# An attention and two expert layers in one kernel: a longer hand-set order, queries turned in other banks, and routings spread over their periods

## The chip, the core and the metric

The kernel runs on one core of a Trainium2 chip. The metric is the device time of one execution in microseconds (us), and less is better. The core has four engines that compute: TensorE (PE in the profile, with its weight loads listed apart as PEld), VectorE (DVE), ScalarE (ACT) and GpSimd (POOL). SyncE (SP) mostly issues transfers. Each engine runs its own instructions strictly in the order of its queue and waits at semaphores for the others.

## The reference, cut to what matters

A recurrent attention over 4 batches, 8 heads, 768 steps and 48 values to a head is followed by two layers of experts over the 3072 tokens that come out of it. Each token goes to one of eight experts; nothing is dropped.

```python
for t in range(768):                       # for every batch and head
    y[:, :, t] = r[t] @ (state + outer(u * k[t], v[t]))
    state = w[t][:, None] * state + outer(k[t], v[t])

x = y, heads side by side: 3072 tokens x 384
# layer 1: the router is a cosine
logits = normed(x) @ normed(expert_emb).T / tau
e = argmax(logits); gate = softmax(logits)[e]
x = gate * (relu(x @ w1[e]) @ w2[e])       # 384 -> 1024 -> 384
# layer 2: the router is linear, with a sigmoid gate on top
e = argmax(x @ w_gate); gate = softmax(x @ w_gate)[e]
out = gate * sigmoid(x @ w_output_gate)[e] * (relu(x @ m2w1[e]) @ m2w2[e])
```

## The kernel before, in words

**Attention.** Two heads of one batch make a pair, so there are 16 pairs, g = 0 to 15. Steps lie 6 to a partition. The decays of a pair are turned by six TensorE transposes (`turned`, L590, tile ptw), copied by ScalarE into a padded tile ws (L598), and VectorE runs two product scans over ws, Q (L604) and P (L606): running products of the decays inside chunks of 128 steps. Keys are turned (ptk) and divided by Q into K, queries are turned (ptr) and multiplied by P into R (`scaled`, L616). K scaled by the product of a chunk is Kh (L624). Scores pa = R'Kh (L635) are masked into A (L641), chunk states ps (L658) are chained into sa (L661), the outputs py (L673 with A, L677 with the states) and the bonus term cv give the token rows x (L682). The bonus is cb (L558, a sum of the products rk), which goes to HBM and comes back turned as ct (L559 to L561, cd is its place in HBM), and cv is v times ct on GpSimd (L574).

**Periods.** The pairs are worked on in periods that overlap three pairs. `period(i)` (L759) turns and scans the decays of pair i+1, makes the scores and states of pair i, and finishes the outputs of pair i-1. `period(-1)` is the start, periods 0 to 15 are full ones, and period 16 finishes the last pair. In this text Q(n) is the scan Q of pair n, so that period i runs from the start of Q(i+1) to the start of Q(i+2). The PSUM banks have tags: px (2 banks: everything turned), pa00, pa01, pa40, pa41 (scores, also used for the cosine's turn), py (outputs).

**Router of layer 1.** Whenever 96 columns of x are ready for a batch, the squares of x are summed by ScalarE (`squares`, L691, tile jk), x is turned (L705) and multiplied with the experts' directions (pl, L712), and VectorE adds that into the logits L (L718, L720). After the fourth pair of a batch `route1` (L722) makes the inverse norms on GpSimd (a pow), scales the logits, picks the expert, counts places with a scan and two matmuls (`route`, L311, tile pp), and writes an entry for each token into HBM by six indirect transfers of GpSimd (`scatter`, L367, from the tile ent). For the batches 0 to 2 this lies in periods 5 and 6, 9 and 10, 13 and 14.

**Handover.** `largest` (L406) ranks the experts of the first three batches, the entries of the two first windows are fetched (`entries`, L390, tile first), the raw first weights of the first expert follow (`raw_u`, L397, tile ur_first, four quarters, two buffers), token rows are gathered by indirect transfers (xr, L983), and each weight is split into two parts: a rounded one by ScalarE (uh, vh, L382) and the rest by GpSimd or VectorE (ul, vl, L384).

**Experts.** A unit is a window of up to 512 tokens of one expert. Its matrix products take three passes over the rounded and remaining parts: ph (L1015) in the first product, pz (L1037 and L1048) in the second. Units follow from the handover to the end of the kernel.

**What sets the order.** From the start to the end of period 16 the order of every engine's instructions is that of the code (`tc.manual_schedule`, closed by `order.close()`); from the last batch's routing and the first unit on a scheduler orders, with `queue_behind(x, y)` keeping x behind y.

## Time and profile before

| what | value |
|---|---|
| time, median of 3 runs | 812.99 us (811.99 to 816.59) |
| the profiled execution: own time, span | 808.58 us, 806.9 us |
| TensorE busy | 729.5 us, 90% of the span |
| VectorE busy | 452.9 us, 56% |
| ScalarE busy | 340.6 us, 42% |
| GpSimd busy | 361.5 us, 45% |
| mean granted TensorE clock | 0.941 of full speed |

The span is what the profiler saw between the first and the last instruction; the execution's own time is longer by what lies around it, 1.7 us. An engine's share of busy time is a mean over stages that differ: the attention, the handover and the experts each have their own, and the experts' stage is the longest.

Three views are shown below. A row of a timeline has the start in us, the length in us, the engine and line, the instruction as output <- inputs with sizes, how many follow one another as one row, and in brackets the idle time of the engine ahead of it and what ended that. A row of busy time by stretch has from:to, the length of the stretch, then the busy us (and instructions) of PE, PEld, DVE, ACT and POOL, and last the granted TensorE clock, the share of transfer engines that were busy, and GB/s. The tile view has the instructions that touch one tile, shortest/middle/longest in ns, first and last start.

### The profile page before, as it was taken

To read this page: it belongs to the slowest core of one execution; us is meant where nothing else is said; L and a number is where in the kernel's file an instruction comes from. 1 tells how busy PE (TensorE), PEld (TensorE's weight loads), DVE (VectorE), ACT (ScalarE), POOL (GpSimd) and SP (SyncE) were. 2 spreads that over 40 slices of the span, in tenths; PEclk is the share of its full clock that TensorE was granted. 3 is DMA by queue.
4 is the path that set the end of the run, shared out by engine and by line. 5 is a ranking of instruction groups with operands and counts; after the bars stand their busy time and mean duration, and the time that the engine had idled before them with its cause. 6 is when DMAs were issued, how large, how long until landed. Compare 5 with 4: busy or idle time off the path is not lost.

```text
span 806.9 us, 14112 instructions
## 1 busy us (share of the span) xinstructions
PE 729.5 (90%) x4964; PEld 693.5 (86%) x4964; DVE 452.9 (56%) x1251; ACT 340.6 (42%) x789; POOL 361.5 (45%) x340
## 2 busy tenths in 40 slices
PE   7589969968967888999999999999899999999995
PEld 6578758867856888999999999998898999999995
DVE  6478757767864367688655755754534242342440
ACT  2244634534532363355534434425255353453541
POOL 3342425426333465366525535415365544445530
PEclk9799968979986599999999999999999999999998
DMA  8855634833200645276543553306266342644430
GB/s 175 154 104 87 151 60 61 174 64 47 75 2 3 191 124 151 86 217 207 177 155 98 181 162 113 129 30 192 73 217 198 112 147 93 195 138 149 151 123 19
DMA packets 184052, 100.52 MB, mean 125 GB/s; under 512 B 129373, under 2 KB 180094, under 8 KB 183972
## 3 DMA queue, kind: packets, MB, share of 16 engines
q1 hardware_dynamic: 175504, 83.11, 38.7%
q0 software_dynamic: 7072, 16.04, 6.9%
q8 instruction: 41, 0.67, 0.4%
q10 hardware_dynamic: 1396, 0.38, 0.2%
q14 instruction: 39, 0.32, 0.1%
HBM read 84.01 MB, written 15.95 MB: 124 GB/s over the span
## 4 chain that ended last, share of the span: by engine, by line
PE 56%; issue 12%; DVE 11%; ACT 9%; POOL 5%; DMA 5%; SPq 1%; POOLq 0%; ACTq 0%; DVEq 0%
PE ph L1015 24%; PE pz L1048 12%; PE pz L1037 10%; DVE Q L604 3%; DMA vr<-in_moe_w_dram 3%; ACT Kh L624 2%; PE pq L1001 2%; PE pt L1068 2%; DVE sa L661 2%; DVE K L616 1%; ACT ws L598 1%; POOL reg L367 1%; PE py L673 1%; PE warm L756 1%; ACT jk L691 1%
## 5 line engine op out<-in xcount | busy, mean ns | idle before, releaser
L384 POOL TENSOR_TENSOR ul<-ur,uh 128x768 fp32r<-128x768 f32 x64 | 118.9, 1859 | 139.1 <-ACT uh L382 136.3
L1022 DVE SCALAR_TENSOR_TENSOR hl<-ph,hh 128x256 fp32r<-128x256 f32 (+11 forms) x152 | 79.4, 523 | 128.2 <-ACT hh L1020 127.1
L1015 PE MATMUL ph<-xl,uh 128*128 128x256 f32 (+11 forms) x432 | 143.1, 331 | 0.2 <-DVE xl L1004 0.2
L1015 PE MATMUL ph<-xh,uh 128*128 128x256 f32 (+11 forms) x432 | 142.1, 335 | 0.7 <-ACT xh L1003 0.6
L1015 PE MATMUL ph<-xh,ul 128*128 128x256 f32 (+11 forms) x432 | 142.1, 329 | 0.0
L1020 ACT ACTIVATE hh<-ph 128x256 fp32r<-128x256 f32 (+11 forms) x152 | 70.1, 462 | 91.6 <-PE ph L1015 91.3
L384 DVE TENSOR_TENSOR vl<-vr,vh 128x768 fp32r<-128x768 f32 x66 | 69.6, 1065 | 37.9 <-ACT vh L382 37.5
L1015 PEld LDWEIGHTS ph<-xh,uh 128*128 128x128 f32 x432 | 82.0, 191 | 2.9 <-ACT xh L1003 0.8
L1015 PEld LDWEIGHTS ph<-xl,uh 128*128 128x128 f32 x432 | 82.6, 191 | 2.0 <-DVE xl L1004 0.5
L1015 PEld LDWEIGHTS ph<-xh,ul 128*128 128x128 f32 x432 | 82.7, 191 | 1.7
L673 PE MATMUL py<-v,A 128*128 128x96 f32 x384 | 65.0, 305 | 15.7 <-DVE x L682 10.2
L382 ACT CAST uh<-ur 128x768 fp32r<-128x768 f32 x64 | 53.4, 834 | 55.5 <-PE ph L1015 33.3
L1037 PE MATMUL pz<-hl,vh 128*128 128x256 f32 (+6 forms) x240 | 75.5, 322 | 0.8 <-DVE hl L1022 0.8
L1048 PE MATMUL pz<-vh,hh 128*128 128x384 f32 (+4 forms) x224 | 75.8, 343 | 0.0
L1048 PE MATMUL pz<-vl,hh 128*128 128x384 f32 (+4 forms) x224 | 73.9, 336 | 0.6 <-DVE vl L384 0.6
L1037 PE MATMUL pz<-hh,vl 128*128 128x256 f32 (+6 forms) x240 | 74.2, 317 | 0.0
L673 PEld LDWEIGHTS py<-v,A 128*128 128x128 f32 x384 | 57.5, 220 | 17.0 <-DVE x L682 10.8
L1037 PE MATMUL pz<-hh,vh 128*128 128x256 f32 (+6 forms) x240 | 71.9, 321 | 0.0
L1048 PE MATMUL pz<-vh,hl 128*128 128x384 f32 (+4 forms) x224 | 71.3, 336 | 0.0
L382 ACT CAST vh<-vr 128x768 fp32r<-128x768 f32 x68 | 56.0, 836 | 31.6 <-DMA vr<-in_moe_w_dram 31.0
L624 ACT ACTIVATE Kh<-K,rta 128x128 f32<-128x128 f32 x96 | 31.6, 399 | 76.2 <-DVE rta L621 76.2
L1004 DVE TENSOR_TENSOR xl<-pq,xh 128x384 fp32r<-128x384 f32 x57 | 30.8, 551 | 36.8 <-ACT xh L1003 32.8
(255 smaller groups left out, 1507.9 us busy)
## 6 DMA issues: line engine op xcount, KB each, us to landing
vr<-in_moe_w_dram SPq DMA_DIRECT2D x68, 384.0 KB, 5.8
ur<-in_moe_w_dram SPq DMA_DIRECT2D x64, 384.0 KB, 3.5
wr<-in_w_dram SPq DMA_DIRECT2D x32, 144.0 KB, 3.4
kr<-in_k_dram SPq DMA_DIRECT2D x32, 144.0 KB, 3.3
rr<-in_r_dram SPq DMA_DIRECT2D x32, 144.0 KB, 3.3
v<-in_v_dram SPq DMA_DIRECT2D x32, 144.0 KB, 3.3
xd<-x SPq DMA_DIRECT2D x4, 1152.0 KB, 5.3
yd<-yr SPq DMA_DIRECT2D x3, 768.0 KB, 5.2
```

The source lines that it names most:

```text
L382: nc.scalar.copy(hi, rw)
L384: eng.tensor_tensor(lo, rw, hi.bitcast(F32), ALU.subtract)
L604: nc.vector.tensor_tensor_scan(Q[:, ::-1], x[:, 2:][:, ::-1], rb[:, ::-1], 0.0, ALU.mult, ALU.max)
L624: nc.scalar.activation(st["Kh", g][:, ck(c)], st["K", g][:, ck(c)], AF.Copy, scale=rt[:, c : c + 1])
L661: nc.vector.scalar_tensor_tensor(sa[:M, z], sa[:M, z - 1], st["pt", g][:M, z : z + 1], ps[:M, z], ALU.mult, ALU.add)
L673: nc.tensor.matmul(p[:, c - c0, h].rearrange("p i d -> p (i d)"), A[:, c, h], V[:, c].rearrange("p h d -> p (h d)"), start=c == c0 and h = ...
L1004: nc.vector.tensor_tensor(xl[:, :, tt], p, xh.bitcast(F32)[:, :, tt], ALU.subtract)
L1015: mm = nc.tensor.matmul(p, self.u[f // 2][x][:, o, 128 * (f % 2) : 128 * (f % 2) + 128], self.xs[y][:, o, :n], start=i == 0, stop=i == 8)
L1020: nc.scalar.activation(hh, p, AF.Relu)
L1022: nc.vector.scalar_tensor_tensor(hl, p, 0.0, hh.bitcast(F32), ALU.max, ALU.subtract)
L1037: nc.tensor.matmul(p, self.v[f // 2][x][:, f % 2, o * 128 : (o + 1) * 128], self.h[f][y], start=i == 0, stop=i == 23)
L1048: nc.tensor.matmul(p[:m], self.h[f][x][:, 128 * t : 128 * t + m], self.v[f // 2][y][:, f % 2], start=i == 0, stop=i == 23)
```

## The change

1. The queries are turned into the score banks pa00 and pa01 where they were turned into px.
2. The check that the decays lie below one (`over_one`, jw, L546) moves on ScalarE from the end of a period to right behind the copies ws.
3. `route1` becomes a generator whose steps `period` calls at five places, with the last of its scatters in the next period (`late`). Division by tau moves into the experts' directions, the small copies of the counts move to ScalarE, and the copies of the choice and the place fall away, since these are written straight into keep and ent.
4. At the start, the transfers of constants leave ScalarE's queue, pair 0's inputs are issued from SP and ScalarE both, constants move behind period -1, the bonus of one pair at a time is worked on, the directions are made in steps over periods 0 to 2, and the transposes without use (`warm`) stand in other places, some now in period 0.
5. At the handover, ranking, entries and raw weights are called inside period 15 (`first_units`, the hook), there are four buffers of raw first weights (two before), and the last batch's turn and routing (`opening`) and the first unit are in the hand-set order too, which closes behind the first unit. Small copies of layer 2's entries wait for the unit's rows; the final check of the decays moves to the end.

```diff
-    def route(which, nm, pool, ppool, ptag, L, T, t0, valid, off, tok):
+    def route(which, nm, pool, ppool, ptag, L, T, t0, valid, off, tok, out=None, pad=None, small=nc.vector.tensor_copy):
...
+        small(carry[which], cu[:, :, T])
...
+        pos = mk[:, :, 1]
...
+    UR = 4
...
-                nc.scalar.dma_start(reg.rearrange("(p t) d -> p t d", p=128), none[:, : RP * E // 128])
...
+                nc.sync.dma_start(reg.rearrange("(p t) d -> p t d", p=128), none[:, : RP * E // 128])
...
-                    nc.sync.dma_start(t[nm][:, :, h, :D], src[b, h0 + h].rearrange("(p j) d -> p j d", j=J))
+                    eng = nc.scalar if g == 0 and h else nc.sync
+                    eng.dma_start(t[nm][:, :, h, :D], src[b, h0 + h].rearrange("(p j) d -> p j d", j=J))
...
-        def turned(g, nm):
+        def turned(g, nm, pool=px_p, tags=("px", "px")):
...
-                p = px_p.tile([128, 3, 128], F32, name=f"pt{nm}{g}_{j0}", tag="px")
+                p = pool.tile([128, 3, 128], F32, name=f"pt{nm}{g}_{j0}", tag=tags[j0 // 3], padded_shape=None if pool is px_p else [128, 4, 128])
...
-        def route1(b, spool, stag):
+        def route1(b, pool, tag, pad=None):
             x, ss, L = st["x", b], st["ss", b], st["L", b]
             s1 = ss[:, 0]
             nc.gpsimd.tensor_tensor(s1, s1, ss[:, 1], ALU.add)
             nc.gpsimd.tensor_tensor(s1, s1, half[:, :NC], ALU.pow)
+            yield
             nc.vector.tensor_scalar(s1, s1, 1e-6, None, ALU.add)
             nc.vector.reciprocal(s1, s1)
-            nc.vector.tensor_scalar(s1, s1, itau, None, ALU.mult)
             nc.vector.tensor_tensor(L, L, b3(s1, E), ALU.mult)
-            gate, oh, ii = yield from route(0, f"a{b}", rt_p, spool, stag, L, NC, b * NC, None, None, None)
             ent = st["ent", b]
-            nc.vector.tensor_copy(ent[:, :, 2], gate)
+            gate, oh, ii = yield from route(0, f"a{b}", rt_p, pool, tag, L, NC, b * NC, None, None, None, ent[:, :, 2], pad, nc.scalar.copy)
             yield
             for c in range(NC):
                 scatter("sc1", reg1, ii[:, c : c + 1], ent[:, c], E * RP1)
...
+        def steps_of(g, n):
+            for i in range(n):
+                next(g, None)
...
-        def period(i, bonus, route=iter(())):
+        def period(i, bonus, route=iter(()), late=iter(()), hook=None):
...
+            steps_of(route, 1)
             if n < G:
                 decays(n)
+                over_one(n)
...
+            steps_of(late, 2)
+            if i == 0:
+                warm(8)
...
+            if hook is not None:
+                hook()
...
-                scaled(n, turned(n, "r"), "R", "P", 3)
-                over_one(n)
+                scaled(n, turned(n, "r", pa_p, ("pa00", "pa01")), "R", "P", 3)
...
-            drain(route)
+            steps_of(late, 2)
+            steps_of(route, 6 if i == G - 2 else 2)
...
+        def first_units():
+            ei1, *o1 = largest(0, py_p, "py")
+            evs[:] = [nc.sync.value_load(ei1[0:1, i : i + 1], min_val=0, max_val=E - 1) for i in range(EARLY[0][0])]
+            firsts[:] = [entries(cp, f"first{i}", 1, reg1, ev * RP1, EARLY[0][1] // 128) for i, ev in enumerate(evs)]
+            st["o1"] = o1
+            st["ur"] = raw_u("0_first", evs[0], w1)
...
+    def opening():
+        g = route1(B - 1, px_p, "px")
+        next(g)
+        next(g)
+        yield
+        e0.u += [(uh[q], part_lo(wpu, "u", f"0_first{q}", st["ur"][q], uh[q], [128, NDC, 256], 4, nc.vector)) for q in range(2, 4)]
+        yield
+        next(g)
+        yield
+        drain(g)
+        yield
+        e0.v = []
+        for q in range(4):
+            e0.part_v(q)
...
+        if n == 0:
+            order.close()
+            nxt.after = un.last_mm
```

Three places where instructions move follow, each as it stood and as it stands now; a row is a line, an instruction with output and inputs, and a size. The first is ScalarE's queue from its start to the first copies of decays ws of pair 0. Before:

```order
L834 ACTIVATE okt<-mone 128x1
L836 DMA u_bc<-in_u_dram 128x384
L510 DMA emb<-in_moe_expert_emb_dram 8x384
L512 DMA tau_bc<-in_moe_tau_dram 128x1
L501 DMA reg_60<-none 128x128
L501 DMA reg_61<-none 128x160
L505 DMA xd<-zero 1x384
L505 DMA yd<-zero 1x384
L598 ACTIVATE ws_135<-ptw_0_287 128x128x3
L598 ACTIVATE ws_135<-ptw_3_291 128x128x3
```

The same queue after the change, up to the check of the decays jw of pair 0:

```order
L858 ACTIVATE okt<-mone 128x1
L548 DMA wr_120<-in_w_dram 128x6x48
L548 DMA kr_129<-in_k_dram 128x6x48
L548 DMA rr_124<-in_r_dram 128x6x48
L860 DMA u_bc<-in_u_dram 128x384
L609 ACTIVATE ws_134<-ptw_0_216 128x128x3
L609 ACTIVATE ws_134<-ptw_3_220 128x128x3
L557 ACTIVATE jw_226,wov<-wr_120,mone 128x576
```

The transfers of the directions, of tau and of the zeros no longer stand ahead of ws, three of pair 0's own inputs do, and jw stands right behind ws.

The second is TensorE's queue where period 1 ends and period 2 starts, from the turn of the queries ptr to the turn of the next decays ptw and the first score pa; the semaphores that a row waits for stand in brackets (DVE's here count instructions of VectorE). Before:

```order
L590 MATMUL ptr_0_692<-ident,rr_127 128x128 [waits DMAHW4_49,DMAHW3_49,PE_49]
L590 MATMUL ptr_0_692<-ident,rr_127 128x128 x2
L590 MATMUL ptr_3_696<-ident,rr_127 128x128 [waits PE_49]
L590 MATMUL ptr_3_696<-ident,rr_127 128x128 x2
L590 MATMUL ptw_0_716<-ident,wr_124 128x128 [waits DMAHW7_49,DMAHW0_49,DVE_49]
L590 MATMUL ptw_0_716<-ident,wr_124 128x128 x2
L590 MATMUL ptw_3_720<-ident,wr_124 128x128 [waits DVE_49]
L590 MATMUL ptw_3_720<-ident,wr_124 128x128 x2
L635 MATMUL pa_0_0_737<-R_700,Kh_642 128x128
```

After the change:

```order
L601 MATMUL ptr_0_664<-ident,rr_126 128x128 [waits DMAHW6_49,DMAHW5_49,DVE_49]
L601 MATMUL ptr_0_664<-ident,rr_126 128x128 x2
L601 MATMUL ptr_3_668<-ident,rr_126 128x128 [waits DVE_49]
L601 MATMUL ptr_3_668<-ident,rr_126 128x128 x2
L601 MATMUL ptw_0_694<-ident,wr_123 128x128 [waits DMAHW6_49,DMAHW5_49,PE_49]
L601 MATMUL ptw_0_694<-ident,wr_123 128x128 x2
L601 MATMUL ptw_3_698<-ident,wr_123 128x128 [waits PE_49]
L601 MATMUL ptw_3_698<-ident,wr_123 128x128 x2
L646 MATMUL pa_0_0_717<-R_672,Kh_614 128x128 [waits DVE_49]
```

The order is the same. The turn of the decays waited for VectorE, which frees the px banks by reading ptr out of them; it now waits for TensorE and the inputs alone, and the first score waits for VectorE.

The third is VectorE's queue in period 6, where batch 0 is routed (names with _a belong to the routing; cu is the count, pos the place, ent the entries, A the masked scores, x the token rows). Before, the count stands ahead of the scan Q, and the places and entries behind the last chunk states sa and ahead of the last rows x:

```order
L324 TENSOR_TENSOR D_a_1357<-sc_a_1353,m_a_1355 128x6x8
L328 SCALAR_TENSOR_TENSOR cu_a_1360<-rst_86,D_a_1357 128x56
L604 SCALAR_TENSOR_TENSOR Q_1381<-ws_136,rb 128x768
L606 SCALAR_TENSOR_TENSOR P_1383<-ws_136,rm 128x768
L616 TENSOR_TENSOR K_1432<-ptk_0_1408,Q_1381 128x128x3
...
L661 SCALAR_TENSOR_TENSOR sa_1460<-sa_1460,pt_1198,ps_1459 112x96 x4
L335 TENSOR_SCALAR base_a_1473<-m_a_1355 128x6
L339 TENSOR_TENSOR tmp_a_1475<-pp_a_1416,D_a_1357 128x48
L341 TENSOR_REDUCE pos_a_1477<-tmp_a_1475 128x6
L352 COPY keep_87<-pos_a_1477 128x6
L733 COPY ent_246<-gate_a_1486 128x6
L682 TENSOR_TENSOR x_1005<-py_4_1494,cv_1341 128x2x96
```

After the change:

```order
L693 TENSOR_TENSOR x_1156<-py_2_1390,cv_1324 128x2x96
L740 TENSOR_SCALAR ss_917<-ss_917 128x6
L741 RECIPROCAL ss_917<-ss_917 128x6
L742 TENSOR_TENSOR L_918<-L_918,ss_917 128x48
...
L324 TENSOR_TENSOR D_a_1419<-sc_a_1416,keep_87 128x6x8
L328 SCALAR_TENSOR_TENSOR cu_a_1422<-rst_86,D_a_1419 128x56
L652 TENSOR_TENSOR A_1359<-pa_0_0_1360,upper 128x4x128
...
L627 TENSOR_TENSOR R_1477<-ptr_3_1473,P_1351 128x128x3
L336 TENSOR_TENSOR tmp_a_1481<-pp_a_1461,D_a_1419 128x48
L338 TENSOR_REDUCE keep_87<-tmp_a_1481 128x6
...
L297 RECIPROCAL ent_536<-gate_a_1492 128x6
L615 SCALAR_TENSOR_TENSOR Q_1525<-ws_134,rb 128x768
```

The scaling of the logits and the count now stand behind the rows x of the middle of the period, and the places and entries behind R, at the period's end, ahead of the next scan Q.

## Rows read from the trace of the kernel before

**Rows 1.** The page's first line.

```profile
span 806.9 us, 14112 instructions
```

**Rows 2.** Busy time by engine in a stretch of the experts.

```profile
340.00:380.00 40.00, 39.82 (x322) 39.42 (x321) 33.08 (x106) 21.64 (x47) 26.59 (x21) 1.00 0.69 211
```

**Rows 3.** Timeline of VectorE, scans Q: start, us, instruction, idle before and releaser.

```profile
10.01 1.76 DVE L604 TENSOR_TENSOR_SCAN Q<-ws,rb 128x768 f32<-128x768 f32 x1 [3.10 <-ACT ws L598]
...
38.96 1.76 DVE L604 TENSOR_TENSOR_SCAN Q<-ws,rb 128x768 f32<-128x768 f32 x1 [1.89 <-ACT ws L598]
52.37 1.76 DVE L604 TENSOR_TENSOR_SCAN Q<-ws,rb 128x768 f32<-128x768 f32 x1 [1.26 <-ACT ws L598]
...
231.71 1.73 DVE L604 TENSOR_TENSOR_SCAN Q<-ws,rb 128x768 f32<-128x768 f32 x1
```

**Rows 4.** Busy time in periods 2 to 6, one to a row, columns as in rows 2.

```profile
52.37:64.31 11.94, 9.72 (x95) 8.65 (x95) 9.89 (x20) 5.40 (x15) 4.37 (x5) 1.00 0.57 103
64.31:76.79 12.48, 11.86 (x113) 10.58 (x112) 10.01 (x21) 6.07 (x18) 4.83 (x8) 1.00 0.56 97
76.79:90.21 13.42, 12.80 (x126) 11.39 (x125) 10.01 (x21) 8.73 (x30) 4.38 (x5) 1.00 0.58 97
90.21:106.51 16.30, 12.98 (x117) 11.29 (x116) 12.09 (x32) 8.04 (x29) 5.95 (x7) 1.00 0.76 168
106.51:126.38 19.87, 14.05 (x79) 12.63 (x81) 11.71 (x33) 5.69 (x16) 7.65 (x9) 0.57 0.20 38
```

**Rows 5.** Timeline of all engines where period 2 ends; columns as in rows 3.

```profile
62.02 1.02 DVE L616 TENSOR_TENSOR R<-ptr,P 128x384 f32<-128x384 f32 x2
...
62.62 1.01 PE L590 MATMUL ptw<-ident,wr 128*128 128x128 f32 x6 [1.18 <-DVE R L616]
...
63.27 0.57 ACT L598 ACTIVATE ws<-ptw 128x384 f32<-128x384 f32 x1 [0.32 <-PE ptw L590]
```

**Rows 6.** Timeline, TensorE's turn of queries in period 3, ScalarE's check in period 4.

```profile
73.85 0.85 PE L590 MATMUL ptr<-ident,rr 128*128 128x128 f32 x6
...
86.94 0.78 ACT L546 ACTIVATE jw<-wr,mone 128x576 f32<-128x576 f32 x1
```

**Rows 7.** Timeline of VectorE, two instructions of the routing in periods 5 and 6.

```profile
104.14 0.17 DVE L727 TENSOR_SCALAR ss<-ss 128x6 f32<-128x6 f32 x1 [2.72 <-POOL ss L726]
...
119.78 0.20 DVE L339 TENSOR_TENSOR tmp_a<-pp_a,D_a 128x48 f32<-128x48 f32 x1
```

**Rows 8.** Timeline of the handover on three engines.

```profile
253.49 0.97 POOL L367 DMA_INDIRECT reg<-ent,ii_a  x1 [0.30 <-issue]
...
260.52 0.40 SPq L390 DMA_DIRECT2D first<-reg  x1
...
285.94 0.37 PE L1015 MATMUL ph<-xh,uh_first 128*128 128x256 f32 x1
...
309.17 0.28 PE L1015 MATMUL ph<-xh,uh 128*128 128x256 f32 x1
```

**Rows 9.** Timeline of ScalarE and VectorE at the start.

```profile
8.96 0.57 ACT L598 ACTIVATE ws<-ptw 128x384 f32<-128x384 f32 x1 [6.64 <-DMA reg<-none]
...
33.83 0.75 DVE L558 TENSOR_REDUCE cb<-rk 128x12 f32<-128x576 f32 x1 [3.00 <-POOL rk L555]
```

**Rows 10.** Tile view of the raw first weights: issues, casts, times to landing.

```profile
L397 SPq DMA_DIRECT2D ur_first<-in_moe_w_dram x4: 372/372/373, 261.7 to 275.5; - x4
L382 ACT CAST uh_first<-ur_first x4: 826/830/832, 270.9 to 282.9; 128x768 fp32r<-128x768 f32 x4
...
DMA to landing us min/median/max: 3.6/3.7/3.8
```

**Rows 11.** Busy time in stretches of the handover, columns as in rows 2.

```profile
272.00:276.00 4.00, 4.00 (x21) 4.00 (x21) 0.77 (x2) 2.32 (x8) 3.45 (x2) 0.50 0.27 80
...
280.00:284.00 4.00, 4.00 (x40) 4.00 (x39) 1.25 (x5) 2.21 (x7) 0.15 (x1) 1.00 0.66 236
```

**Rows 12.** Timeline of TensorE, the transposes without use at the handover.

```profile
273.83 5.17 PE L756 MATMUL warm<-ident 128*128 128x128 f32 x24
```

More of the change, by code (lines that the diff above doesn't have):

```diff
@@ L803, in period @@
                 sources_first(i, 1)
+                if p < 0:
+                    warm(8)
                 states(i)
-            next(route, None)
+                if p < 0:
+                    warm(16)
+            if router and not mid:
+                cosine_sum(b2, q2 - 1, pa_p, "pa40")
+                cosine_add(b2, q2 - 1)
             if p >= 0:
```

290 lines of the change are left out of this document (151 added, 139 removed).

## The prediction

> **What bounds the kernel now.** I read the page first, for the span of 806.9 us [rows 1], then busy time by stretch, then the timelines of the places where VectorE or TensorE waits. In the experts' stage TensorE is full: 39.82 of 40 us at the whole clock [rows 2]. The change takes no matmul out of it, so what can shrink lies ahead of the second unit of the experts.
>
> That stretch falls into three. The start reaches to Q(3) at 52.37, the periods from there to Q(15) at 231.71 take 179.34 [rows 3], and the handover follows, to the second unit.
>
> No engine is full in the periods. In period 2 VectorE works 9.89 and TensorE 9.72 of 11.94 us [rows 4]; VectorE's largest idle time is ahead of Q, 1.26, and it waits there for the copy ws [rows 3]. The reader sees why in the timeline: VectorE reads the turned queries into R from 62.02, TensorE's turn of the next decays waits 1.18 for that, the copy waits for the turn, and the scan for the copy [rows 5]. VectorE so waits for a chain that its own R holds up. Periods 3 to 5 add router work, 12.48, 13.42 and 16.30 us; period 6, which routes a batch, takes 19.87 with the granted clock at 0.57 [rows 4], near the lower of TensorE's two levels (1.2 of 2.4 GHz).
>
> **The turn of the queries.** With the queries in the score banks, which the masks read long before, the turn of the decays need not wait for R. In period 2 the whole 1.26 goes: 11.94 - 1.26 = 10.7. The stall is not lost altogether: the next first score needs R and now waits where the turn waited. R ends at 62.02 + 1.02 = 63.04, and the turn, moved up, is done by about 62.4, so TensorE idles about 0.6 there; the scores feed a mask that stands behind two scans on VectorE (1.76 + 1.73 [rows 3]) and K, which covers it. 10.7 leaves VectorE 0.8 idle beside its 9.89. Bounds: nothing, if R or another reader holds the chain as before, and 2.05 (11.94 - 9.89).
>
> In period 3 TensorE is nearly full (11.86 of 12.48 [rows 4]). Its turn of the queries starts at 73.85 and takes 0.85 [rows 6]; the decays' turn follows for another 0.85, the second half of ws takes 0.57 [rows 5], and Q could start at about 76.15, where it started at 76.79 [rows 4]: 11.85.
>
> **The check jw.** In periods with squares ScalarE has jw, 0.78 [rows 6], ahead of ws. Behind ws it delays Kh, which waits for VectorE anyway. 13.42 - 0.77 = 12.65; bounds 0 and 0.78.
>
> **The routing.** Period 5 holds 16.30 - 13.42 = 2.9 us more than period 4, nearly all of it VectorE's wait of 2.72 for the pow on GpSimd [rows 7]. Issued at the start of the next period, the pow has half a period ahead of its reader; period 5 becomes 12.65 too. A batch's three periods then take 11.85 + 12.65 + 12.65 = 37.15 for 42.20. In a routing period VectorE has nine small operations behind the middle rows and eight behind R, at 0.17 to 0.20 [rows 7], with gaps about 2.0 and 1.5 in all, none of which I take as hidden: 10.7 + 2.0 + 1.5 = 14.2 for 19.87. The two matmuls of the count and the exponentials lie beside them. The six scatters of GpSimd, 6 x 1.27 = 7.6 (0.97 + 0.30 [rows 8]), fall at the ends of two periods in which GpSimd works some 4.4 of 11.94 [rows 4], so they are covered; without the cover the bonus product would delay x by at most two of them, 2.5. Bounds of the routing period: 12.7 (the second group covered) and 17.
>
> From Q(3) to Q(15) there are period 2, three batches of three and two routing periods: 10.7 + 3 x 37.15 + 2 x 14.2 = 150.55, a gain of 28.8.
>
> **The start.** ScalarE's first copy ws waits 6.64 behind issues of transfers, until the last zeros for the registers [rows 9], and VectorE waits 3.10 of that at Q(0), 10.01 [rows 3]. The inputs of pair 0 are issued from two queues; I take the 3.1 whole. The inputs' own time to land bounds it: 0 to 3.1. The Trainium skill ("DMA: Bandwidth & Descriptors", Issuing engines are not separate DMA queues) says that several issuers save only the issue time; the 3.1 is an issue wait, and the trace does not show whether landing then takes its place.
>
> Q(0) to Q(2) takes 28.95 [rows 3]. Two periods without foreign work are 21.4; the copies' wait of 1.89 [rows 3] and the wait of 3.00 for the second bonus [rows 9] go for certain. So the gain is between 4.9 and 7.55; constants now behind period -1 partly still stand there: 22, a gain of 7. Period 1 takes 52.37 - 38.96 = 13.41, gain between 1.26 and 2.7, I take 1.8 (11.6). Sum of the start: 11.9, bounds 3.2 (waits for ws alone, 1.89 + 1.26) and 13.4.
>
> **The handover.** Call Q(15) T. Now the last scatter of batch 2 is at 253.49 = T + 21.8, the fetch of entries is issued 7.03 later, the raw weights 1.2 after it at 261.7 and land in 3.7, yet ScalarE casts the first quarter at 270.9 and the last, whose raw buffer came free late, at 282.9 [rows 8, 10]. The first product is at 285.94 = T + 54.2, the second unit's at 309.17, 23.2 later and 77.46 behind T [rows 3, 8].
>
> After: entries stand at the end of the routing period, T + 14.2; six scatters at 1.27 put the last at T + 20.7, the fetch at T + 27.7, the weights at T + 28.9, landed at T + 32.6. Two casts (0.83 each [rows 10]) lead to T + 34.3, and about ten instructions of period 16 and of the rows' split stand between on ScalarE, 0.5 each by the row of ws: first product at T + 39.5. The unit is 144 matmuls; at 39.82 / 322 = 0.124 [rows 2] that is 17.8, and I take 21, since weights and routing still come in between. While it waits TensorE falls to the lower level: rows of that sort show 21 matmuls in 4 us where the full level does 40 [rows 11], and about 5 us of that cost 2.3. T + 62.8, a gain of 14.5. Bounds: 5, if only the idle 270.9 - 265.4 before the first cast goes, and 20 (T + 57.3, no loss in the unit).
>
> **The rest.** The experts: nothing; the small copies lie on VectorE, 33.08 of 40 busy [rows 2]. The final rows one after the other let one scatter less stand behind the last matmul: 0 to 1, I take 0.5.
>
> **Sum.** 11.9 + 28.8 + 14.5 + 0.5 = 55.7 off the profiled execution's own 808.58: 752.9. The median of the runs shown is 0.55% above that execution; on its scale 757.
>
> **The clock, a rule against the row.** From 272 to 276 the clock is at 0.50; 24 transposes without use start at 273.83, and from 280 to 284 it is at 1.00 [rows 11, 12]. So the clock rises while the engine does transposes, and the transposes of the changed start should do the same.
>
> The Trainium skill ("TensorE: Matmul & The Clock Gate", Part 4: PE-mode transpose) says the opposite, that the full clock doesn't engage for transposes because they don't count as busy in the same way. By it the warm transposes now put into the periods would be spent for nothing; by the row they serve. I go by the row.
>
> **The rivals.** (a) As summed, 757, in 740 to 767: 60%.
>
> (b) The handover keeps its length, since the chain of scatters, entries and weights on GpSimd's and SP's queues only moves along with ScalarE's casts: 757 + 14.5 = 772. For it: the chain to T + 32.6 is nearly as long as before (T + 33.7). Against: the 5.5 idle before the first cast and the two raw buffers. 15%.
>
> (c) The periods shrink by the routing alone, as the first scores now hold what the turn held: 12 periods of about 1.2 [rows 5] back, 757 + 14 = 771: 12%. Both (b) and (c): 785, 5%.
>
> (d) Routing covered and the handover at its bound: 735 to 745, 3%.
>
> (e) Slower: TensorE stays at the lower level, since the attention's matmuls have gaps whose fill is transposes. A period at that level is worth 19.87 - 14.2 = 5.7 [rows 4]; it is one mechanism, from the start to the handover, and outweighs the gain from 10 of the 16 periods on; in all 16 it gives 757 + 91 = 848. Against it stand the clocks of 1.00 in periods 2 to 5 [rows 4]. 3%. The rule of the page above speaks for this case.
>
> (f) The change does nothing: the score banks come free as late as px, and the steps of the routing wait for each other as before: about 813, 2%.
>
> **How the numbers follow.** The point is case (a). 742 to 780 leaves out (e), (f), the sum of (b) and (c), part of (d) and the ends of (a). About 0.5% is what a measurement of this kernel can tell from no change. Faster by more: (a) to (d), 0.95; within it (f), 0.02; slower (e), 0.03.
>
> **What the profile after would show.** Right: Q without idle time ahead of it in period 2 and a wait of TensorE ahead of the first score; periods of 10.7, 11.9, 12.7 and 14.2; jw behind ws; the granted clock at 1.00 from 100 to 140; Q(0) near 7, Q(3) near 40.5, Q(15) near 191, the first product near 230, the second unit near 254. Wrong: Q still waiting for ws; VectorE waiting for the exponentials or the count's matmuls; first scores late enough that the masks wait; the first unit's weights landing late; the experts' stretch longer than 497.7 (806.9 - 309.17 [rows 1, 8]), which no step here foresees.

## The result and the profile after

The changed kernel takes 782.55 us, median of 4 runs (779.00 to 787.02), beside 812.7 for the kernel before. The ratio is 0.962, with an interval of 0.956 to 0.968. It is faster, as forecast, but by 30 us and not by 56, and 782.55 lies 2.5 above the upper end of the range. The profiled execution took 779.0, span 777.3; that is 29.6 less than the execution of before.

The stretches of the prediction's sum, from the profiles (Q(n) is the scan Q of pair n; the units' starts are those of their first product ph):

| stretch | before | forecast | after |
|---|---|---|---|
| start to Q(3) | 52.37 | 40.5 | 41.62 |
| Q(3) to Q(15) | 179.34 | 150.55 | 152.40 |
| Q(15) to the second unit | 77.46 | 62.8 | 63.10 |
| second unit to the end | 497.7 | 497.2 | 520.2 |

Three rows came within 2 us. The fourth, to which the prediction gave no change but half a microsecond, holds nearly all of the miss: it is 22.5 us longer than before and 23.0 above the forecast, of 26.3 in all.

The page after, its span:

```profile
span 777.3 us, 14040 instructions
```

The scans Q after, on VectorE's timeline, those that answer to [rows 3]:

```profile
6.98 1.76 DVE L615 TENSOR_TENSOR_SCAN Q<-ws,rb 128x768 f32<-128x768 f32 x1 [3.33 <-ACT ws L609]
...
52.56 1.76 DVE L615 TENSOR_TENSOR_SCAN Q<-ws,rb 128x768 f32<-128x768 f32 x1 [0.20 <-ACT ws L609]
...
194.02 1.76 DVE L615 TENSOR_TENSOR_SCAN Q<-ws,rb 128x768 f32<-128x768 f32 x1 [1.12 <-ACT ws L609]
```

Busy time in periods 2 to 6 after, which answers to [rows 4]:

```profile
41.62:52.56 10.94, 9.34 (x92) 8.46 (x90) 9.96 (x21) 4.78 (x16) 4.36 (x5) 1.00 0.62 115
52.56:64.42 11.86, 11.59 (x119) 11.00 (x119) 10.01 (x21) 6.04 (x18) 4.42 (x5) 1.00 0.83 148
64.42:77.06 12.64, 12.22 (x129) 11.38 (x125) 10.01 (x21) 8.89 (x30) 4.79 (x8) 1.00 0.68 119
77.06:89.38 12.32, 11.45 (x108) 10.31 (x107) 10.01 (x21) 8.07 (x30) 5.14 (x7) 1.00 0.83 195
89.38:104.37 14.99, 11.08 (x103) 9.55 (x103) 14.37 (x36) 6.25 (x20) 5.16 (x6) 1.00 0.46 81
```

Forecast were 10.7, 11.85, 12.65, 12.65 and 14.2. The end of period 2 after, on TensorE's and ScalarE's timelines, shows the step itself:

```profile
50.88 0.87 PE L601 MATMUL ptw<-ident,wr 128*128 128x128 f32 x6
52.33 1.61 PE L646 MATMUL pa<-R,Kh 48*128 48x128 f32 x24 [0.57 <-DVE R L627]
...
51.53 1.00 ACT L609 ACTIVATE ws<-ptw 128x384 f32<-128x384 f32 x2 [0.24 <-PE ptw L601]
52.55 0.78 ACT L557 ACTIVATE jw<-wr,mone 128x576 f32<-128x576 f32 x1
```

The turn of the decays ptw no longer waits, where it waited 1.18 for R [rows 5]. The first score pa waits 0.57 for R in its place (0.6 was forecast), and the check jw stands behind ws.

The handover after, on the timelines of GpSimd, SP, ScalarE and TensorE; it answers to [rows 8, 10]:

```profile
216.46 0.97 POOL L363 DMA_INDIRECT reg<-ent,ii_a  x1 [0.30 <-issue]
...
222.49 0.99 SPq L396 DMA_DIRECT2D first<-reg  x2
223.68 2.73 SPq L403 DMA_DIRECT2D ur_first<-in_moe_w_dram  x4
...
227.74 1.61 ACT L381 CAST uh_first<-ur_first 128x768 fp32r<-128x768 f32 x2
...
235.40 0.58 PE L1047 MATMUL ph<-xh,uh_first 128*128 128x256 f32 x1 [0.96 <-ACT xh L1035]
...
257.12 0.28 PE L1047 MATMUL ph<-xh,uh 128*128 128x256 f32 x1
```

Behind Q(15), the last scatter is at 22.4, the entries at 28.5, the weights at 29.7, the first cast at 33.7 and the first product at 41.4; forecast were 20.7, 27.7, 28.9, 32.6 (the landing) and 39.5. The first unit then takes 21.7, where 21 and 2.3 for the clock were forecast.

Two stretches of the experts after, busy time by engine; before, TensorE was full in such a stretch [rows 2]:

```profile
300.00:340.00 40.00, 36.21 (x273) 35.09 (x273) 22.77 (x67) 17.85 (x37) 20.69 (x18) 1.00 0.56 180
340.00:380.00 40.00, 36.97 (x215) 36.35 (x215) 26.83 (x84) 16.98 (x33) 15.73 (x14) 1.00 0.41 128
```

TensorE idles 3.8 and 3.0 of 40 us. The units' intervals in us, from the first product of one to that of the next, say where:

| interval of unit | 2 | 4 | 6 | 10 | 11 | 12 | the other twelve, 3 to 19 |
|---|---|---|---|---|---|---|---|
| before | 24.5 | 20.8 | 31.0 | 28.9 | 32.4 | 19.9 | |
| after | 29.1 | 26.1 | 33.8 | 36.9 | 34.8 | 18.4 | each within 0.6 |

Unit 10 is the last of the first layer. The transfers and what waits for them where the layers change, after, on the timelines of SP, GpSimd, TensorE and VectorE (ur and vr are raw weights, xr the gathered rows of the second layer's first unit, pq their turn, ul and vl the remainders of weights, xl that of the rows, pt the rows of unit 10):

```profile
506.46 2.60 SPq L373 DMA_DIRECT2D ur<-in_moe_w_dram  x4
509.26 2.70 SPq L992 DMA_DIRECT2D vr<-in_moe_w_dram  x4
...
508.43 0.99 POOL L1013 DMA_INDIRECT xr<-yd,mt  x1 [5.34 <-issue]
...
514.80 0.55 PE L1031 MATMUL pq<-ident,xr 128*128 128x128 f32 x3 [2.25 <-DMA xr<-yd,mt]
...
511.96 7.11 POOL L386 TENSOR_TENSOR ul<-ur,uh 128x768 fp32r<-128x768 f32 x4
517.03 3.73 DVE L386 TENSOR_TENSOR vl<-vr,vh 128x768 fp32r<-128x768 f32 x2 [0.23 <-ACT vh L381]
...
521.28 1.81 PE L1100 MATMUL pt<-iw,yT 128*128 128x144 f32 x6 [3.46 <-DVE xl L1036]
```

The same place before, on the timelines of SP, GpSimd and TensorE:

```profile
544.43 9.44 SPq L377 DMA_DIRECT2D ur<-in_moe_w_dram  x4
554.07 2.08 SPq L377 DMA_DIRECT2D vr<-in_moe_w_dram  x4
...
546.32 0.98 POOL L983 DMA_INDIRECT xr<-yd,mt  x1 [5.39 <-issue]
...
550.39 0.87 PE L1001 MATMUL pq<-ident,xr 128*128 128x128 f32 x6
552.09 0.55 PE L1001 MATMUL pq<-ident,xr 128*128 128x128 f32 x3 [0.82 <-DVE xl L1004]
```

Before, the four issues of ur take 9.44: the third comes at 551.73, when a raw buffer is free, so that the gathers run beside two weight transfers. TensorE turns the gathered rows at 550.39, 4.1 behind the first gather's issue, without waiting for them. After, with four buffers, eight weight transfers of 384 KB are issued in 5.5 us around the gathers (506.46 to 511.96), and TensorE waits for the first rows until 514.80, 6.4 behind the issue. Then VectorE makes two remainders vl, 3.73, ahead of the remainder xl for which TensorE waits 3.46. Two such remainders take 1.81 right after (at 521.15). The first of these took 2.87 and ended at 519.90, 0.8 behind the last of four remainders ul that GpSimd made in a row, at 519.07.

In the second unit casts of weights (vh) that have not landed stand on ScalarE in front of due work, and VectorE waits behind them. On the timelines of ScalarE, TensorE and VectorE, after (yT is the copy of a unit's product):

```profile
261.59 0.83 ACT L381 CAST vh<-vr 128x768 fp32r<-128x768 f32 x1 [2.73 <-DMA vr<-in_moe_w_dram]
277.26 0.83 ACT L381 CAST vh<-vr 128x768 fp32r<-128x768 f32 x1 [5.32 <-DMA vr<-in_moe_w_dram]
...
263.57 3.25 PE L1100 MATMUL pt<-iw,yT 128*128 128x144 f32 x12 [3.90 <-ACT yT L1071]
...
278.12 0.96 DVE L386 TENSOR_TENSOR vl<-vr,vh 128x768 fp32r<-128x768 f32 x1 [5.38 <-ACT vh L381]
```

At 261.59 ScalarE has stood 2.73 for a weight, and yT, for which TensorE waits 3.90, is queued behind it; before, TensorE waited 2.39 at that place. At 277.26 ScalarE has stood 5.32 for a weight of the third unit and VectorE 5.38 for its cast; the hidden values hh and hl, which the second unit's second product needs, are queued behind, and TensorE waits 1.61 and 0.64 for them. It works 22.9 of the unit's 29.1 us, before 22.0 of 24.5. In the sixth unit it is the same: ScalarE stands 6.75 for a weight (cast at 365.55) and TensorE 3.03 for yT, where it had no such wait before. In the fourth, TensorE waits 1.18 for a count on VectorE (a scan, cu, that took 1.84 beside a remainder on GpSimd where it takes 0.21 elsewhere) and 1.89 for xl, which stands behind an instruction for which VectorE waits 3.42 until a scatter lands.

### The profile page after: what moved, and what is told of

The parts are those of the page before. It is cut to its first block, busy times and chain, and to the rows that moved or that the text cites. A ratio compares the mean times of both kernels' runs of the same rounds, so it can differ in the third digit from the quotient of the medians.

```text
span 777.3 us, 14040 instructions
## 1 busy us (share of the span) xinstructions
PE 711.6 (92%) x4928; PEld 679.3 (87%) x4928; DVE 449.4 (58%) x1196; ACT 340.4 (44%) x799; POOL 353.8 (46%) x335
## 4 chain that ended last, share of the span: by engine, by line
PE 51%; DVE 14%; issue 13%; DMA 9%; ACT 7%; POOL 4%; SPq 2%; POOLq 0%; ACTq 0%; DVEq 0%
PE ph L1047 20%; PE pz L1080 12%; PE pz L1069 7%; DMA vr<-in_moe_w_dram 5%; DVE Q L615 3%; PE py L684 2%; ACT Kh L635 2%; PE pq L1031 2%; DVE sa L672 2%; DVE K L627 2%; POOL ul L386 1%; PE pt L1100 1%; ACT ws L609 1%; DMA ur<-in_moe_w_dram 1%; PE ps L669 1%
## 5 line engine op out<-in xcount | busy, mean ns | idle before, releaser
L1036 DVE TENSOR_TENSOR xl<-pq,xh 128x384 fp32r<-128x384 f32 x57 | 30.7, 553 | 58.5 <-ACT xh L1035 41.9
L363 POOL DMA_INDIRECT reg<-en,ii x29 | 29.4, 1015 | 65.7 <-DVE ii L347 58.6
L684 PE MATMUL py<-v,A 128*128 128x96 f32 x384 | 59.1, 286 | 0.0
L635 ACT ACTIVATE Kh<-K,rta 128x128 f32<-128x128 f32 x96 | 31.6, 399 | 57.5 <-DVE rta L632 57.5
```

Source lines behind the costliest of these rows:

```text
L363: x = nc.gpsimd.indirect_dma_start(dst, bass.IndirectOffsetOnAxis(ap=idx, axis=0), src, None, bounds_check=rows - 1, oob_is_err=False).ins
L635: nc.scalar.activation(st["Kh", g][:, ck(c)], st["K", g][:, ck(c)], AF.Copy, scale=rt[:, c : c + 1])
L684: nc.tensor.matmul(p[:, c - c0, h].rearrange("p i d -> p (i d)"), A[:, c, h], V[:, c].rearrange("p h d -> p (h d)"), start=c == c0 and h = ...
L1036: nc.vector.tensor_tensor(xl[:, :, tt], p, xh.bitcast(F32)[:, :, tt], ALU.subtract)
```

## The experiments

Theory T: the four raw buffers (`UR`) cost the experts what they lost. With them, a later unit's transfers go out in one burst, and the planned order puts casts and remainders of weights that have not landed in front of work that is due. Rival S: the order behind the first unit is planned anew because its start is another, and the buffers have no part in it. Rival R: the rules that hold the second unit's casts back cost the second unit's 4.7. All kernels below were timed beside the kernel before; the spans and stretches are those of one profiled execution each.

Profiles of equal code say how much a stretch varies by itself. From Q(3) to Q(15) four kernels with equal code, the changed one among them, take 152.4 to 152.5, and others 153.8, 154.7 and twice 156.0. They differ in two places alone: period 2 takes 10.9 at a granted clock of 1.00 or 13.2 at 0.87, period 11 takes 12.4 at 0.86 to 1.00 or 13.7 at 0.80. The experts' stretch with four buffers is 517.2 to 520.2 where nothing there was edited, that with two 500.0 to 502.0.

**Two buffers.**

```diff
-    UR = 4
+    UR = 2
```

> Two raw buffers for the first weights instead of four, for the first unit and for every later one; all else as changed. Theory T (the fourth buffer lets a later unit's eight weight transfers go out in one burst, ahead of or beside the small gathers, and puts the casts of late weights in front of work that is due): from the second unit's first product to the end, 520.2 us after the change against 497.7 before, comes back to 498 to 505; the handover from Q(15) to the first unit's first product, 41.4, grows by 2 to 6, since the last two quarters wait for a cast again; time 763 to 772. Rival S (the order behind the first unit is simply planned anew from another start, and two buffers leave that as it is): 515 to 525 for that stretch, and the time is 780 to 790.

762.5 us, ratio 0.936 (0.930 to 0.943). From the second unit on, 259.11 to 761.1, it is 502.0. T holds, S falls. Q(15) is at 196.28 and the first product at 238.16, 41.9 later: that is 0.5 more than in the changed kernel and not 2 to 6, so that part of the expectation failed.

**Four for the first unit, then two.** The first unit's quarters 2 and 3 get a tag of their own:

```diff
-            rw = wpu.tile([128, NDC, 256], F32, name=f"ur{nm}{q}", tag="ur", bufs=UR)
+            rw = wpu.tile([128, NDC, 256], F32, name=f"ur{nm}{q}", tag=("ur", "urf")[q // 2], bufs=UR)
...
-    UR = 4
+    UR = 2
```

> Four raw buffers for the first unit, two for every later unit, in the same space as the changed kernel. Theory T: the handover stays at 41 to 42 from Q(15) to the first product, the experts' stretch behind the second unit's first product comes to 498 to 505, and the time is 758 to 768, the fastest so far. Rival S: experts' stretch 515 to 525, time 778 to 788.

761.7 us, ratio 0.936 (0.929 to 0.942); stretch 500.6. A stretch of its experts, and the change of layers on the timelines of SP, GpSimd and TensorE:

```profile
300.00:340.00 40.00, 39.86 (x296) 39.24 (x295) 34.91 (x103) 19.97 (x44) 25.57 (x20) 1.00 0.63 191
```

```profile
495.71 9.38 SPq L373 DMA_DIRECT2D ur<-in_moe_w_dram  x4
...
500.12 0.95 POOL L1013 DMA_INDIRECT xr<-yd,mt  x1 [0.30 <-DMA ur<-in_moe_w_dram]
...
501.65 0.82 PE L1031 MATMUL pq<-ident,xr 128*128 128x128 f32 x6
```

TensorE is full again, the issues take 9.38 as before, and the turn waits for no gather. The first product is 42.8 behind Q(15), no earlier than with two: four buffers bring the handover nothing.

**The kernel before with four.**

```diff
-            rw = wpu.tile([128, NDC, 256], F32, name=f"ur{nm}{q}", tag="ur", bufs=2)
+            rw = wpu.tile([128, NDC, 256], F32, name=f"ur{nm}{q}", tag="ur", bufs=4)
...
-        return [split(wpu, "u", f"{nm}{q}", m1[bass.ds(ev, 1), :, 256 * q : 256 * q + 256].rearrange("x (o p) f -> p (x o) f", p=128), [128, NDC, 256], 4)
+        return [split(wpu, "u", f"{nm}{q}", m1[bass.ds(ev, 1), :, 256 * q : 256 * q + 256].rearrange("x (o p) f -> p (x o) f", p=128), [128, NDC, 256], 4, 4)
```

> The kernel before with four raw buffers for the first weights in place of two, and nothing else. Theory T: its experts' stretch grows from 497.7 to 508 to 522, mostly at the second to sixth unit and where the layers change; the handover shortens by 2 to 8; time 815 to 830. Rival S: the stretch moves by less than 5, and the time is 803 to 815 by the handover alone.

833.98 us, ratio 1.024 (1.017 to 1.031): longer by more than the noise; whether by 2% is open. Its stretch from the second unit's first product at 316.99 is 519.7, beside 497.7, with 28.0, 27.2 and 37.0 in the second, fourth and tenth unit. In these three units that is the changed kernel's loss, in a kernel without the rest of the change (the sixth, with 31.6, loses little here); TensorE's timeline has the same two waits where the layers change:

```profile
573.75 0.55 PE L1001 MATMUL pq<-ident,xr 128*128 128x128 f32 x3 [2.57 <-DMA xr<-yd,mt]
...
580.11 1.81 PE L1068 MATMUL pt<-iw,yT 128*128 128x144 f32 x6 [2.85 <-DVE xl L1004]
```

The handover did not shorten here either (56.2 from Q(15) to the first product, before 54.2).

**Casts not held.**

```diff
-            nxt.after = un.last_mm
...
-            if n == 0:
-                for x in casts[-4:]:
-                    queue_behind(x, un.last_act)
```

> The changed kernel without the two rules that hold the second unit's casts behind the first unit's last ReLU and its first turn behind the first unit's last product. Theory T: the loss at the change of layers (7.9) and in the fourth and sixth unit (5.3, 2.8) stays, so the experts' stretch stays at 515 to 523. Rival R (the added rules cost the second unit its 4.7): the second unit's interval falls from 29.2 to 25 or less, the stretch to about 515, and the time falls by 4 to 5.

783.56 us, ratio 0.964 (0.956 to 0.972); stretch 524.2, just above the range, second unit 31.1. R falls: the rules do not cost the second unit its time.

**Two at the change of layers.** Four for all units, as two tags of two; the first of the second layer takes one tag alone, so two.

```diff
-        rw = pool.tile(sh, F32, name=f"{tag}r{nm}", tag=f"{tag}r", bufs=raws)
+        rw = pool.tile(sh, F32, name=f"{tag}r{nm}", tag="urf" if nm[-1] in "23" and nm[:5] != "1_0_0" else f"{tag}r", bufs=raws)
...
-    UR = 4
+    UR = 2
...
-            rw = wpu.tile([128, NDC, 256], F32, name=f"ur{nm}{q}", tag="ur", bufs=UR)
+            rw = wpu.tile([128, NDC, 256], F32, name=f"ur{nm}{q}", tag=("ur", "urf")[q // 2], bufs=UR)
```

> Four raw buffers for all units but the first one of the second layer, which has two. If the burst of that unit's transfers beside the gather of its rows is what the tenth unit loses, the tenth unit falls from 36.9 to 29 to 31 and the other losses (second unit 29.1, fourth 26.1, sixth 33.8) stay: stretch 511 to 515, time 772 to 778. If the plan of the whole stretch moves at random with such edits, other units' intervals change by over 2 too.

776.75 us, ratio 0.959 (0.954 to 0.963). The tenth unit takes 29.4 for 36.9, the fourth and sixth keep 26.1 and 33.3; the second grows to 32.3, so other units do move, by up to 3.2. The stretch is 517.0, 3.2 below 520.2, where 5 to 9 were expected: the tenth unit gives 7.5, the second takes 3.2 of it, the twelfth 3.9 (22.3 for 18.4).

**Three buffers.**

```diff
-    UR = 4
+    UR = 3
```

> Three raw buffers for all units. If each transfer more in flight costs alike, the experts' stretch lies between those of two (502) and four (520): 508 to 514. If only the four quarters of a unit going out as one burst matter, it is 500 to 504.

766.66 us, ratio 0.948 (0.942 to 0.953); stretch 508.1, at the edge of the first form. The cost grows with the buffers: 502.0, 508.1, 520.2. The tenth unit takes 29.4, 32.8 and 36.9.

**All casts held, four buffers.** In every unit the next unit's casts (`casts`) are kept behind the last hidden values hh on ScalarE, and their remainders on VectorE (`lows`) behind the last hl (`last_dve`).

```diff
-            if n == 0:
-                for x in casts[-4:]:
-                    queue_behind(x, un.last_act)
             nxt.wv()
+            for x in casts[-8:]:
+                queue_behind(x, un.last_act)
+            for x in lows[-4:]:
+                queue_behind(x, un.last_dve)
```

> The changed kernel, four raw buffers throughout, with every unit's casts of weights on ScalarE and their remainders on VectorE held behind the last ReLU parts of the unit before it. Two forms of the theory of the fourth buffer are told apart. Order (early transfers let the plan put the next unit's casts in front of work that is due): the second unit falls from 29.1 to 25.5 or less, the fourth from 26.1 to 22.5 or less, the tenth, ahead of the change of layers, from 36.9 to 33, since only the wait behind the remainders (3.5) goes there; the experts' stretch comes to 503 to 512. Burst (the transfers themselves come late because all are under way at once): nothing changes, 516 to 524.

806.36 us, ratio 0.995 (0.992 to 0.998), 23.8 above the changed kernel's median. The second unit falls from 29.1 to 25.9, nearly as the order form has it, but the fourth rises from 26.1 to 38.6 and the stretch to 547.6. Neither form foresaw that. Its fourth unit, on VectorE's, GpSimd's and TensorE's timelines:

```profile
302.06 7.07 DVE L386 TENSOR_TENSOR vl<-vr,vh 128x768 fp32r<-128x768 f32 x4
303.87 3.56 POOL L386 TENSOR_TENSOR ul<-ur,uh 128x768 fp32r<-128x768 f32 x2
...
309.75 1.78 PE L1102 MATMUL pt<-iw,yT 128*128 128x144 f32 x6 [6.24 <-DVE xl L1038]
...
328.38 7.17 POOL L386 TENSOR_TENSOR ul<-ur,uh 128x768 fp32r<-128x768 f32 x4
328.50 7.88 DVE L386 TENSOR_TENSOR vl<-vr,vh 128x768 fp32r<-128x768 f32 x1 [1.15 <-ACT vh L381]
```

All four remainders now stand in one piece of 7.07 ahead of xl, and TensorE waits 6.24. Four of them take VectorE 3.8 by themselves; here the third took 4.47, from 303.80 to 308.27, and ended 0.8 behind two remainders of GpSimd (at 307.43). The next remainder took 7.88 beside four of GpSimd's and ended 0.8 behind them too, and TensorE waited 7.57 at 339.50 for the xl behind it. In the whole kernel 24 of VectorE's 68 remainders took over 1.2, in the changed one 4. So the place of these instructions costs time with no transfer edited: due work stands behind them, and they stand beside GpSimd's. Holding them late is only another wrong place.

**Queries back in px.**

```diff
-                scaled(n, turned(n, "r", pa_p, ("pa00", "pa01")), "R", "P", 3)
+                scaled(n, turned(n, "r"), "R", "P", 3)
```

> The changed kernel with the queries turned in the px banks as before; all else as changed. If the step of the prediction holds (the turn of the next decays then waits for R again, 1.2 us in each of some 12 periods), the stretch from Q(3) to Q(15), 152.4 after the change, comes to 160 to 168, TensorE's turn of the decays shows a wait of about 1.2 for R in plain periods, and the time is 790 to 800. Rival: the wait moved to the first score costs as much as the one removed; then the stretch stays within 3 of 152.4.

788.04 us, ratio 0.971 (0.965 to 0.977). Q(3) to Q(15) is 40.19 to 199.38, 159.2 for 152.4: 6.8, just below the 7.6 to 15.6 expected. Of the 6.8, 4.3 lie in periods 2 and 11, where profiles of equal code differ too; the other ten periods hold 2.5, 0.6 to 0.7 in each of periods 3 and 7 and at most 0.2 in periods 4, 5, 8, 9, 12 and 13. On the whole time the kernel cannot be told from the changed one. The wait is back, 0.90 on TensorE and 1.18 ahead of Q, in period 2's end:

```profile
51.28 1.01 PE L601 MATMUL ptw<-ident,wr 128*128 128x128 f32 x6 [0.90 <-DVE R L627]
...
52.95 1.76 DVE L615 TENSOR_TENSOR_SCAN Q<-ws,rb 128x768 f32<-128x768 f32 x1 [1.18 <-ACT ws L609]
```

**The check back at the period's end.**

```diff
                 decays(n)
-                over_one(n)
                 scans(n)
...
                 scaled(n, turned(n, "r", pa_p, ("pa00", "pa01")), "R", "P", 3)
+                over_one(n)
```

> The changed kernel with the check of the decays at the end of a period on ScalarE, ahead of the next copies, as before. By the prediction six periods with squares lose 0.77 each, so Q(3) to Q(15) grows by 4.6; as the copies are now due earlier in the other periods too, up to 0.5 more in each of six: 157 to 160. Rival: TensorE is nearly full in these periods (12.22 of 12.64 in period 4), so that the check costs nothing there: within 1 of 152.4.

784.64 us, ratio 0.967 (0.961 to 0.973). Q(3) to Q(15) is 41.21 to 199.10, 157.9: 5.5 more. The six periods with squares take 0.8 more each, 4.7 in all, as the prediction had it, and period 2 takes 0.6 more. The step holds; on the whole time it cannot be told from the changed kernel.

**No transposes without use.**

```diff
         def warm(n):
+            return
```

> The changed kernel without the transposes that have no use, at the start and in period 0; nothing of the result depends on them. By the row of the profile before (the granted clock rose from 0.50 to 1.00 while 24 such transposes ran), they hold the clock up: without them the granted clock from 0 to 41 falls from 0.92 to 0.6 to 0.8 and Q(3), 41.6, comes 2 to 8 later. By the rule that transposes do not count as busy they change nothing: the clock stays at 0.92 within 0.05 and Q(3) within 1, or earlier by the time that they took.

776.08 us, ratio 0.957 (0.951 to 0.963), not told from the changed kernel's; of the 3.7 us by which its span is shorter, 3.0 lie in the experts' stretch, which the edit doesn't touch. Q(3) is at 41.13, within 1 of 41.62, as the rule had it. The granted clock's column reads 1.00 from 0 to 42 in this kernel, which neither side expected, but the lengths of equal turns say otherwise. The turn of six keys on TensorE's timeline without these transposes (they are called the fill below):

```profile
6.51 1.51 PE L601 MATMUL ptk<-ident,kr 128*128 128x128 f32 x6 [0.58 <-DMA kr<-in_k_dram]
...
30.11 1.51 PE L601 MATMUL ptk<-ident,kr 128*128 128x128 f32 x6
...
41.34 0.87 PE L601 MATMUL ptk<-ident,kr 128*128 128x128 f32 x6
```

and with them, in the changed kernel:

```profile
7.81 0.82 PE L601 MATMUL ptk<-ident,kr 128*128 128x128 f32 x6
```

Six turns take 0.82 with the fill and 1.51 without it, at 6.51 and still at 30.11. So the transposes do bring TensorE to its full pace early. It is worth nothing here, since what they save they cost: without them period 1, Q(2) to Q(3), takes 13.1 for 11.4, but Q(0) to Q(2) takes 21.5 for 23.3 (21.8 to 23.2 in other kernels with the same code there). There, in the changed kernel, VectorE waits 1.12 for the turn of the queries (R at 28.55), which is queued behind 16 of these transposes of 3.30.

**Squares behind the next copies.** In the kernel with four buffers then two; the routing's step at a period's start moves behind the scans with them.

```diff
-            steps_of(route, 1)
             if n < G:
                 decays(n)
+                for x in st.pop("pend", ()):
+                    squares(*x)
                 over_one(n)
                 scans(n)
+            steps_of(route, 1)
...
-            if sq:
-                squares(b2, q2 - 2, range(3 if mid else 0, NC))
+            if sq and mid:
+                st["pend"] = [(b2, q2 - 2, range(3, NC))]
+            elif sq:
+                squares(b2, q2 - 2)
```

> Four raw buffers for the first unit and two later, and on ScalarE the second half of a batch's squares moved from the end of a period to behind the next period's copies of decays, since Q waits 1.43 and 1.11 for these copies in periods with squares. If ScalarE's order alone holds these six periods, each falls by 1.1 to 1.4, and Q(3) to Q(15) shrinks by 6 to 8 against the kernel with four buffers then two; if TensorE holds them (12.22 of 12.64 and 11.45 of 12.32 busy after the change), by 1 to 4. Time 755 to 761.

759.5 us, ratio 0.934 (0.929 to 0.940), Q(3) to Q(15) 154.2 beside 156.0 with four buffers then two. Periods 4 and 5 fall from 12.6 and 12.3 to 11.85 each, but period 6 grows from 15.0 to 16.6: the pow behind the squares ends at 95.08, and the first routing operation on VectorE (ss, at 95.11) now stands beside GpSimd's product rk and takes 1.38, where it took 0.16. Over the batches the six periods lose 3.8 and the two routing periods take 3.2 back. The 1.8 lies in the expected 1 to 4, but 1.2 of it is in period 11, by the difference that equal code shows there.

**Together:** four then two, squares later, no fill.

> Four raw buffers for the first unit and two later, squares behind the next copies, and no transposes without use. By the parts (759.5 with the squares moved; the transposes' removal took the profiled span of the changed kernel from 777.3 to 773.6): 754 to 760. If the transposes of the first periods serve the clock after all in this version: 760 to 766.

759.54 us, ratio 0.938 (0.934 to 0.941), in the first form's 754 to 760, but no less than with the squares alone: the 3.7 that the expectation took from the missing fill did not come. The two best versions, 759.5 and 759.5, are some 23 us below the changed kernel.

## Why the prediction was wrong

**The step that failed** is "The experts: nothing". It named the small copies on VectorE as the only thing to cost there, and took the four raw buffers as a gain of the handover alone. `UR` is also the count for every later unit's first weights, by `load_u`, which the list of the change leaves out. Shown: with two buffers the stretch is 502.0, in the kernel before with four it is 519.7. That is 18 to 22 us of the 22.5. What remains with two buffers against 497.7, some 2 to 4 us, lies mostly in the twelfth unit (22.5 for 19.9); the runs do not tell its cause. Among its signs of being wrong the prediction had a stretch longer than 497.7, with no step for it.

How a buffer more loses time was followed at two units. At the change of layers the burst makes the gather late and the remainders stand in front of xl; two buffers for that unit alone take 7.5 off the tenth unit. In the second and sixth unit ScalarE, and VectorE behind it, stands at casts of weights that have not landed, with due work queued behind. That the plan expected the weights earlier than they land is argued from the order, not shown by itself. Which part is the transfers and which the order is not settled.

A third part is likely and was not tested by itself: with four buffers GpSimd makes four remainders ul in a row at the change of layers, with three buffers three and with with two never more than two, and an instruction of VectorE's beside such a row can end as late as the row. In the tenth unit this is at most 1.9 us, the excess of the remainder at 517.03; in the kernel with all casts held it is 3.5 and 6.9 around the fourth unit.

**The start**: 10.75 gained, 11.9 forecast. The first copy ws starts at 5.93, where it started at 8.96 [rows 9], and Q(0) is at 6.98, near 7 as forecast. VectorE still waits 3.33 there, since it arrives earlier too. The copy now waits for the turn of the decays, and without the fill that turn waits until 4.41 for its input to land: landing has taken part of the issues' place, which the prediction left open. The miss lies in Q(0) to Q(2), 23.3 for 22, where VectorE waits 1.12 behind the transposes without use (the fill).

**The periods**: 26.9 gained, 28.8 forecast. The largest misses are the routing periods, 15.0 for 14.2, and periods 7 and 11, 12.4 for 11.85; periods 5, 9 and 13 came 0.3 shorter than forecast. The sum was nearly right while one price behind it was not: undoing the queries alone costs 6.8 or less, where the case in which the score's wait takes the turn's place put 14. In the periods with squares next to nothing comes back, and TensorE is nearly full there (12.22 of 12.64 in period 4). The check costs 4.7 in the periods with squares, where 4.6 was put. The routing is dearer than its 0.17 to 0.20 an operation [rows 7]: two of step 2's operations took 1.20 and 0.84 us in period 6, beside GpSimd (rows in the last section), and the prediction counted no wait on GpSimd there.

**The handover**: 14.4 gained, 14.5 forecast, in part by luck: the first product came 1.9 later than forecast and the first unit took 1.6 less. The chain of scatters, entries and weights gave nothing, as case (b) had it: the last scatter is 22.4 behind Q(15) and the weights are issued at 29.7, where they were at 21.8 and 30.0 [rows 8, 10]. The gain lies behind the chain. The first cast comes at 33.7 where it came at 39.2, and the first product 7.7 behind that cast where it came 15.0 behind it. The raw buffers, named against case (b), had no part in it: 41.9 with two, 42.8 with four then two, 41.4 in the changed kernel. What remains of the change there is the hand-set order of the last batch's routing and the first unit; no run takes that back by itself.

**The clock**: the row was right against the rule, though on the time of Q(3) the rule's outcome came. The Trainium skill ("TensorE: Matmul & The Clock Gate", Part 4: PE-mode transpose) says that the full clock doesn't engage for transposes; six turns took 0.82 behind such transposes and 1.51 without them, and the measurement decides.

**The rivals**: of the slower rival, (e), nothing came: the granted clock is 1.00 in periods 2 to 6, and 0.96 over 100 to 140. (c) and (b) did not come either, although 782.55 is near their sum of 785: the time agreed with a case whose two mechanisms are both refuted by the table of stretches.

## What to carry to other kernels

Look up every user of a constant that a change raises. A deeper buffer is not a free gain: it lets transfers start together and lets an ordering program put their readers early, and an engine that works strictly in order then stands at a late transfer with due work behind it. Before a difference of a stretch is put down to an edit, look how far that stretch differs between profiles of equal code. When a forecast misses, compare it stretch by stretch, not by the total; three of four terms here were right, and the one at zero was the miss.

## What the runs showed of the hardware

A small VectorE operation can take as long as what is left of the GpSimd one beside it. Step 2 of the routing in period 6 after, and one element's subtraction at the handover, on the timelines of GpSimd and VectorE:

```profile
95.02 1.41 POOL L566 TENSOR_TENSOR rk<-rk,u_bc 128x576 f32<-128x576 f32 x1
96.39 1.15 POOL L585 TENSOR_TENSOR cv<-v,ct 128x576 f32<-128x576 f32 x1
...
95.29 1.20 DVE L742 TENSOR_TENSOR L<-L,ss 128x48 f32<-128x48 f32 x1
96.76 0.84 DVE L282 TENSOR_TENSOR d_a<-L,mx_a 128x48 f32<-128x48 f32 x1
...
254.61 7.19 POOL L386 TENSOR_TENSOR ul<-ur,uh 128x768 fp32r<-128x768 f32 x4
253.98 7.85 DVE L964 TENSOR_TENSOR fit<-fit,lh 128x1 f32<-128x1 f32 x1
```

The product with two operands, 48 elements, ends at 96.49 where rk ends at 96.43, and the difference at 97.60 where cv ends at 97.54; the reduction between them takes its 0.20. The subtraction of one element a partition, fit, takes 7.85 and ends at 261.83, where four remainders of GpSimd end at 261.80. The other way round, cv took 3.29 at 41.22, beside the scans Q and P, in the kernel with four buffers then two, and 1.16 at 50.89; its period 2 took 13.2 where the changed kernel's took 10.9, and why cv stood beside the scans there is not known. The Trainium skill ("SBUF — State Buffer", Who interferes with whom) says that a VectorE instruction with two inputs in SBUF and a GpSimd one that reads SBUF share a port under an exclusive lock; these rows agree.

The page's granted clock can read 1.00 while TensorE works at half pace: without the fill the column is at 1.00 from 0 to 42, and six turns take 1.51 up to 30.11 and 0.87 at 41.34.
